# Moving the block transpose of head 16 behind the second MLP half of batch 0, and that of head 17 and the hash of heads 14 to 17 a little later

## The chip, the cores and the metric

One core of a Trainium2 chip runs the kernel. The metric is device time of one execution in microseconds (us), the median of several runs. A profile's span is some 1.8 us shorter than the time of the same run. Each run also lists the mean clock that was granted to TensorE (1.0 is full speed).

TensorE is the matmul engine, VectorE and ScalarE work on elements, GpSimd does elementwise work here, slowly (2.13 us for one `scale` of 128 x 768 elements), and SyncE only issues transfers, in order, from one queue.

## The reference, cut to what matters

```python
def _attn_ref(q, k, v, proj):              # batch 4, 8 heads, 768 positions, head size 64
    q_bucket, k_bucket = ...               # 6-bit hash of each row of q and of k, by the signs of x @ proj
    scores = scale * q @ k.T               # masked to -1e9 where the two buckets differ
    return softmax(scores) @ v

def _moe_ref(x, w_in, w_out):              # 3072 tokens, 512 -> 2048 -> 512
    h = x @ w_in
    return (h * cos(h)) @ w_out
```

So attention is followed by a dense MLP. The kernel numbers the heads of all batches 0 to 31; batch 0 is heads 0 to 7, batch 1 heads 8 to 15, batch 2 heads 16 to 23.

## The kernel before: the parts that matter

The program is one fixed interleaving of all work. Step `s` does the scores of slot `s` and the attention sums of slot `s - 1`, in nine units. Other work is hung onto this clock by `at(time, f, ...)`: 10.5 means behind unit 4 of step 10. This orders the instructions of every engine's queue; it sets no time.

```python
    PREP.update({hd: hd - 5.6 for hd in range(16, 28)})
    PREP[16] = 10.5                                  # head 17: 11.4
    HASH = {10: 8.2, 14: 12.4, 18: 16.4, ...}        # cut
    ...
    for m in range(8, NH // 2):                      # loads of heads 2m and 2m+1
        at(9.05 if m == 8 else PREP[2 * m] - 2.6, load_qk, m)      # SyncE queue
        at(9.1 if m == 8 else PREP[2 * m] - 2.4, load_v, m)
    for hd in range(H, NH):
        at(SCALE.get(hd, PREP[hd]), scale, hd, nc.vector if hd == 8 else nc.gpsimd)
        at(PREP[hd], blocks, hd)                     # VectorE
        at({...}.get(hd, SCALE.get(hd, PREP[hd]) + 0.12), turn, hd)   # DMA transpose, SyncE queue
```

`blocks(hd)` is one VectorE transpose in 32 x 32 blocks of the loaded q and k; only the hash reads its result. `scale(hd)` makes a bf16 copy on GpSimd, which `turn(hd)` transposes by DMA. The hash of four heads is 16 small matmuls.

Twice per batch, at the head of a step, stands an MLP half. For batch 0 the second one, `hidden(0, 1)`, opens step 11:

```python
    def hidden(b, c, pools):                         # pools: ps_o (2 buffers) and ps_st (3), in turn
        for ff in range(NFF):                        # 16 groups
            hp = pool.tile([P, 512], FP32, ...)      # PSUM
            for ft in range(NFT): nc.tensor.matmul(out=hp[:, 0:TOK], ...)     # 4 matmuls, 384 columns
            nc.scalar.activation(out=cs, in_=hp[:, 0:TOK], func=ACTF.Sin, ...)
            nc.vector.tensor_tensor(out=gt, in0=hp[:, 0:TOK], in1=cs, op=ALU.mult)   # the gate

    def normalize(s):                                # VectorE: flat, osum, rec, xtok
        ...                                          # osum reads the last use of a ps_o buffer
```

The two `ps_o` buffers ("o_att") also hold the attention sums. `normalize(9)` stands at the end of step 10, so VectorE gets `blocks(16)` (10.5), then `normalize(9)`, then the 16 gates of `hidden(0, 1)`, in this order.

The softmax here doesn't subtract the row's maximum and nothing guards it: scores larger than these inputs give would overflow.

## Time and profile before

| before | |
|---|---|
| time, median of 3 runs | 314.02 us (313.32 to 314.09) |
| span of the profile | 311.6 us |
| TensorE busy | 300.9 us (97%) |
| span before the second MLP half of batch 0 | 78.16 us |
| this half (16 groups) | 15.43 us |
| span after it | 218.01 us |

The half's limits are the start of its first matmul (line 485) and the start of the first attention matmul behind it (line 371).

TensorE is nearly always busy, so only places where it is not can give much. This is the view of busy time by stretch for the kernel before, cut at the half. Columns: stretch and its length, then busy us (and instructions) of TensorE, its weight loads, VectorE, ScalarE, GpSimd, then granted TensorE clock, DMA share, GB/s.

```profile
78.16:93.59 15.43, 12.40 (x65) 6.81 (x65) 9.66 (x19) 9.30 (x18) 11.29 (x10) 0.89 0.94 253
93.59:311.60 218.01, 213.14 (x1927) 126.74 (x1925) 123.54 (x247) 168.96 (x315) 50.10 (x43) 1.00 0.32 84
```

Three of 15.4 us are idle, and the mean clock is 0.89. The waits between 70 and 100 us (who waited for whom: total, times, longest) say what for:

```profile
DVE qk L224 <- DMA nat_qk<-in_k_dram: 5.7, 1, 5.7
...
ACT cs L493 <- DVE gt L497: 3.1, 1, 3.1
PE o_att L485 <- DVE osum L405: 2.6, 1, 2.6
...
PE st L485 <- DVE gt L497: 0.5, 1, 0.5
```

TensorE (PE) waits for VectorE (DVE), and VectorE for the load of k. VectorE's instructions in order of time (start, us, instruction, and in brackets the idle time before it) show why one transpose matters:

```profile
75.34 0.70 DVE L288 COPY ext<-ext 8x1536 bf16<-8x1536 bf16 x1
81.73 0.98 DVE L224 STREAM_TRANSPOSE qk<-nat_qk 128x768 f32<-128x768 f32 x1 [5.69 <-DMA nat_qk<-in_k_dram]
82.63 0.19 DVE L403 COPY flat<-o_att 128x65 f32<-128x65 f32 x1
82.86 0.56 DVE L405 TENSOR_TENSOR osum<-o_att,flat 128x390 f32<-128x390 f32 x1
...
84.16 0.55 DVE L497 TENSOR_TENSOR gt<-st,cs 128x384 f16<-128x384 f32 x1
```

The transpose of head 16 waits 5.69 us for its load, and flat, osum and the gates stand behind it. Nothing overtakes. The Trainium skill, "TensorE: Matmul & The Clock Gate" (the table at its head), calls the queues of VectorE, ScalarE and GpSimd "8 strict FIFO"; for VectorE this trace agrees: the attention matmuls that flat reads had ended by 77.1 us, and flat ran at 82.63, behind the transpose.

TensorE's instructions in the same form, and below them the chain of waits (start, us, what):

```profile
79.46 1.46 PE L485 MATMUL st<-xT,win 128*128 128x384 f16 x8
83.47 0.81 PE L485 MATMUL o_att<-xT,win 128*128 128x384 f16 x4 [2.55 <-DVE osum L405]
84.76 1.08 PE L485 MATMUL st<-xT,win 128*128 128x384 f16 x4 [0.48 <-DVE gt L497]
```

```profile
77.26 4.38 DMA nat_qk<-in_k_dram
...
81.73 0.98 DVE qk L224
82.71 0.12 DVE flat L403
...
84.24 0.48 DVE gt L497
...
84.76 1.08 PE st L485 x4
```

Four groups go through; the fifth needs an o_att buffer, which osum must first read. Last, the clock, again by stretch (the third column from the right):

```profile
84.00:85.00 1.00, 0.52 (x4) 0.23 (x3) 1.00 (x3) 0.20 (x1) 1.00 (x2) 1.00 1.05 372
85.00:86.00 1.00, 1.00 (x6) 0.46 (x5) 1.00 (x3) 0.88 (x3) 0.92 (x2) 0.58 1.10 381
86.00:87.00 1.00, 1.00 (x5) 0.50 (x4) 1.00 (x3) 0.37 (x1) 0.87 (x2) 0.50 1.06 246
87.00:88.00 1.00, 1.00 (x5) 0.50 (x4) 0.34 (x2) 0.49 (x1) 0.96 (x1) 0.50 1.27 189
88.00:89.00 1.00, 1.00 (x6) 0.51 (x5) 0.28 (x2) 0.49 (x1) 1.00 (x1) 0.71 0.97 320
```

TensorE counts as fully busy here, but at half speed. Sixteen groups at 0.65 us (four matmuls of 384 columns, back to back) are 10.4 us; 15.43 less 10.4 less 2.55 less 0.48 leaves 2.0 us. Of these, the clock column accounts for some 1.7 (0.42, 0.50, 0.50 and 0.29 of the four stretches from 85 to 89 us).

### The profile page before, as it was taken

The page shows a single profiled execution, that of the slowest core. Times are in us where ns is not written, and L with a number is a line of the kernel's source. Part 1 is how long each engine was busy: PE and PEld are TensorE (multiplying, and loading weights), DVE is VectorE, ACT ScalarE, POOL GpSimd, SP SyncE. Part 2 cuts the span into 40 slices and gives each one's busy share as a digit, 9 for nine tenths or more (in the row PEclk, how much of TensorE's full clock was granted, in tenths as well). Part 3 has the DMA queues.
Part 4 walks back from the last instruction along what each step waited for, and adds up shares of the span by engine and source line. Part 5 has one row for each costly group of instructions (what it writes and reads, how often), then busy time and mean ns, then how long its engine had stood idle before and what let it go on. Part 6 is the DMA issues. An engine that isn't in the chain of part 4 may idle for free.

```text
span 311.6 us, 7060 instructions
## 1 busy us (share of the span) xinstructions
PE 300.9 (97%) x2782; PEld 181.6 (58%) x2782; DVE 190.9 (61%) x371; ACT 243.9 (78%) x457; POOL 125.3 (40%) x134
## 2 busy tenths in 40 slices
PE   8999999999599999999999999999999999999995
PEld 2587665656356565656655656665656655654542
DVE  3788967966478877658856676539851265130720
ACT  3789998989569898997787978998768886942821
POOL 4697996899599357704931830000000000000000
PEclk9999999999989999999999999999999999999999
DMA  6679999956982479349407352340001200123001
GB/s 199 233 138 281 251 178 194 322 111 132 304 197 97 98 218 199 93 84 313 75 2 219 90 86 74 69 108 2 2 0 56 69 32 23 47 54 101 34 36 67
DMA packets 53569, 38.07 MB, mean 122 GB/s; under 512 B 33600, under 2 KB 49312, under 8 KB 53536
## 3 DMA queue, kind: packets, MB, share of 16 engines
q1 hardware_dynamic: 44272, 26.99, 34.2%
q0 software_dynamic: 8320, 10.49, 14.9%
q8 instruction: 22, 0.36, 0.5%
q10 hardware_dynamic: 944, 0.13, 0.3%
q14 instruction: 11, 0.09, 0.1%
HBM read 27.27 MB, written 6.29 MB: 108 GB/s over the span
## 4 chain that ended last, share of the span: by engine, by line
PE 69%; DMA 12%; POOL 10%; issue 3%; SPq 2%; DVE 2%; ACT 1%; POOLq 0%; ACTq 0%; DVEq 0%
PE y L509 22%; PE st L328 13%; PE st L485 12%; PE o_att L485 8%; PE o_att L371 8%; DMA nat_v<-in_v_dram 4%; DMA nat_qk<-in_k_dram 4%; DMA wout<-in_moe_w_out_dram 3%; POOL blk L205 2%; PE tp L509 2%; PE tp L234 2%; POOL vacc L126 2%; POOL v_ext L121 1%; SPq L87 1%; POOL wout L469 1%
## 5 line engine op out<-in xcount | busy, mean ns | idle before, releaser
L336 ACT ACTIVATE pt<-st 128x512 f16<-128x512 f32 x288 | 154.6, 617 | 19.8 <-PE st L328 18.6
L509 PE MATMUL y<-wout,gt 128*128 128x512 f16 x352 | 109.3, 378 | 0.0
L328 PE MATMUL st<-ext 72*128 72x512 bf16 (+3 forms) x480 | 108.0, 294 | 0.9 <-DVE ext L169 0.6
L371 PEld LDWEIGHTS <-pt 128*128 128x128 f16 x1152 | 71.1, 97 | 27.6
L371 PE MATMUL o_att<-v_ext,pt 128*128 128x65 f16 x1152 | 82.1, 193 | 0.0
L485 PEld LDWEIGHTS <-win 128*128 128x128 f16 x512 | 50.6, 99 | 39.3 <-issue 7.5
L205 POOL TENSOR_SCALAR blk<-nat_qk 128x768 bf16<-128x768 f32 x23 | 50.7, 2203 | 41.4 <-DMA nat_qk<-in_k_dram 27.4
L328 PEld LDWEIGHTS <-ext 72*128 72x128 bf16 x480 | 43.9, 97 | 30.3 <-issue 7.3
L485 PE MATMUL st<-xT,win 128*128 128x384 f16 x304 | 59.0, 330 | 0.6 <-DVE gt L497 0.5
L497 DVE TENSOR_TENSOR gt<-st,cs 128x384 f16<-128x384 f32 x76 | 41.7, 555 | 16.9 <-ACT cs L493 12.3
L493 ACT ACTIVATE cs<-st 128x384 f16<-128x384 f32 x76 | 37.1, 491 | 12.5 <-PE st L485 8.9
L485 PE MATMUL o_att<-xT,win 128*128 128x384 f16 x208 | 43.0, 330 | 3.8 <-DVE osum L405 2.6
L509 PEld LDWEIGHTS <-gt 128*128 128x128 f16 x384 | 33.6, 98 | 14.0
L497 DVE TENSOR_TENSOR gt<-o_att,cs 128x384 f16<-128x384 f32 x52 | 28.9, 555 | 12.6 <-ACT cs L493 9.8
L405 DVE TENSOR_TENSOR osum<-o_att,flat 128x390 f32<-128x390 f32 x24 | 13.6, 565 | 33.1 <-PE o_att L371 32.5
L493 ACT ACTIVATE cs<-o_att 128x384 f16<-128x384 f32 x52 | 25.5, 491 | 6.3 <-PE o_att L485 6.2
L224 DVE STREAM_TRANSPOSE qk<-nat_qk 128x768 f32<-128x768 f32 x24 | 23.1, 969 | 5.9 <-DMA nat_qk<-in_k_dram 5.7
L524 ACT COPY o_sb<-y 128x512 f32<-128x512 f32 x22 | 12.8, 583 | 14.6 <-PE y L509 14.6
L126 POOL TENSOR_TENSOR vacc<-nat_v 128x384 f32<-128x384 f32 x16 | 17.0, 1063 | 0.0
L121 POOL CAST v_ext<-nat_v 128x768 f16<-128x768 f32 x16 | 13.6, 848 | 5.9 <-PE o_att L371 2.7
L422 DVE TENSOR_TENSOR xtok<-osum,rec 128x384 f16<-128x384 f32 x24 | 15.3, 638 | 0.9
L169 DVE TENSOR_SCALAR ext<-qk 64x768 bf16<-64x768 f32 x15 | 14.5, 968 | 0.4
(78 smaller groups left out, 183.1 us busy)
## 6 DMA issues: line engine op xcount, KB each, us to landing
out_dram<-o_sb SPq DMA_DIRECT2D x23, 256.0 KB
nat_qk<-in_q_dram SPq DMA_DIRECT2D x10, 384.0 KB
nat_qk<-in_k_dram SPq DMA_DIRECT2D x10, 384.0 KB
nat_v<-in_v_dram SPq DMA_DIRECT2D x10, 384.0 KB
nat_v<-in_v_dram POOLq DMA_DIRECT2D x6, 384.0 KB, 8.5
win<-in_moe_w_in_dram POOLq DMA_DIRECT2D x8, 256.0 KB, 9.7
wout<-in_moe_w_out_dram POOLq DMA_DIRECT2D x8, 256.0 KB, 7.9
nat_qk<-in_q_dram POOLq DMA_DIRECT2D x5, 384.0 KB, 8.6
```

The source lines that it names most:

```text
L121: nc.gpsimd.tensor_copy(out=v_all[:, a:a + 2, 0:SB, 0:D], in_=x.rearrange("p h (t d) -> p h t d", d=D),)
L126: nc.gpsimd.tensor_add(acc, x[:, :, 0:3 * D], x[:, :, 3 * D:6 * D])
L205: engine.tensor_scalar(out=blk[hd].rearrange("p t w d -> p w t d"), in0=nat[hd].rearrange("p w (t d) -> p w t d", d=D), scalar1=QK_PRESCAL ...
L224: nc.vector.transpose(out=f32[hd].rearrange("p w c -> p (w c)"), in_=nat[hd].rearrange("p w c -> p (w c)"),)
L328: nc.tensor.matmul(out=st[:, o:o + n], lhsT=e[:, 1, jt * P:(jt + 1) * P], rhs=e[:, 0, t0 * P + c:t0 * P + c + n], start=True, stop=True,)
L336: nc.scalar.activation(out=pts[s][:, u * UNIT:(u + 1) * UNIT], in_=st, func=ACTF.Exp, bias=EXP_BIAS, scale=EXP_SCALE,)
L371: nc.tensor.matmul(out=o_state[s][:, qt * VW:(qt + 1) * VW], lhsT=pts[s][:, f:f + P], rhs=v_all[:, hd % NV, token(hd // H, jt)], start=(i ...
L422: nc.vector.tensor_tensor(out=xtok[b][:, t0:t0 + nt, h * D:(h + n) * D].rearrange("p t (n d) -> p n t d", n=n), in0=o_ps[:, :, 0:D].rearra ...
L485: nc.tensor.matmul(out=hp[:, 0:TOK], lhsT=win_t[ft][:, ff * P // WC, ff * P % WC:ff * P % WC + P], rhs=xT[b, c][:, ft], start=(ft == 0), s ...
L493: nc.scalar.activation(out=cs, in_=hp[:, 0:TOK], func=ACTF.Sin, bias=math.pi / 2.0, scale=1.0)
L497: nc.vector.tensor_tensor(out=gt, in0=hp[:, 0:TOK], in1=cs, op=ALU.mult)
L509: nc.tensor.matmul(out=y_state[b, t], lhsT=gates[b, c][ff][:, tt * P:(tt + 1) * P], rhs=wout_t[:, ff], start=(ff == 0), stop=(ff == NFF - 1),)
```

## The change

The intent is that nothing in front of the MLP half's normalisation and gates waits for the load of heads 16 and 17. The whole diff:

```diff
     PREP.update({hd: hd - 5.6 for hd in range(16, 28)})
-    PREP[16] = 10.5
+    PREP.update({16: 11.05, 17: 11.5})
     PREP.update({28: 22.0, 29: 22.5, 30: 23.0, 31: 23.5})
     PLACE = {10: 8.3, 11: 8.4, 12: 9.8, 13: 10.0}
-    HASH = {10: 8.2, 14: 12.4, 18: 16.4, 22: 20.4, 26: 23.4, 30: 24.6}
+    HASH = {10: 8.2, 14: 12.7, 18: 16.4, 22: 20.4, 26: 23.4, 30: 24.6}
```

`blocks`, `scale` and `turn` of head 16 go from step 10 into step 11, whose MLP half is emitted before its units. Those of head 17 move by one unit; they, like the hash, stood behind that half already. The hash of 14 to 17 moves from unit 4 to unit 6 of step 12, and with it the placements of its bits and the copies of heads 16 and 17 that must precede them (`split`). No instruction is added or removed; the queues of ScalarE and GpSimd keep their order.

## The prediction

> **What bounds the kernel now.** The page: TensorE 300.9 us busy of a 311.6 us span (97%). By stretches, TensorE is busy from 94 to 276 us but for about 1 us. The one large hole is 78 to 94 us (12.86 us busy of 16), in the second MLP half of batch 0 (line 485, emitted at step 11). There the chain of waits runs through the load of heads 16 and 17: its K half is issued at 77.26 us and lands at 81.7. `blocks(16)` is emitted at step 10.5, so it stands in VectorE's in-order queue ahead of the normalisation of step 9 (flat, osum, rec, xtok) and of every gate multiply. VectorE stands still for 5.69 us until the load lands (waits: "qk L224 <- DMA nat_qk", once), and makes the first gate at 84.16. TensorE has done four groups of the half by about 80.9 and waits 2.55 us for osum, to get an accumulator buffer, and 0.48 us for a gate.
>
> A second cost follows: the granted clock drops to 0.50 to 0.58 from 85 to 88 us and is back at 1.0 by 89. The Trainium skill ("TensorE: Matmul & The Clock Gate", "The HAM clock gate") says that an idle window of about 3.4 us halves the clock and a busy one restores it; this trace agrees (some 3.5 us at half clock, after about 3 us of idle time). The other MLP halves, with idle times of at most 0.5 us, keep 1.0. So this half takes 78.16 to 93.6 = 15.4 us, where 16 groups at 0.65 us make 10.4.
>
> **What the change does.** Nothing is added or removed. `blocks(16)` (0.98 us VectorE), `scale(16)` (2.13 us GpSimd) and its DMA transpose move from step 10.5 to unit 0 of step 11, behind the MLP half in program order; those of head 17 move one unit later; the hash of 14 to 17 (1.43 us TensorE) moves two units, its placements with it. The load keeps its place in its queue and still lands near 81.7; nobody urgent waits for it.
>
> **On the critical path.** Up to about 80.9 us nothing changes. Then osum is done near 78 instead of 83.4, so the fifth group starts at once. The sixth needs the first gate: the first cosine starts at 80.40 behind the table load, 0.49 + 0.56 us make 81.5, a stall of 0.1 to 0.2 us. The clock stays up. The half should end at about 88.8 instead of 93.6: a gain of 4.8 us = 2.55 + 0.48 + about 1.8 of half clock. Given back: 0.98 us of VectorE after the half, where it idles 0.99 us before the next flat, so nothing. Settling head 14 keeps about 1 us of slack behind its later placement. From there on TensorE binds, so the gain should reach the end.
>
> **Prediction:** 309.2 us (-1.5%), range 308.3 to 310.8. Faster by over 2%: 0.03; within 2%: 0.96; slower: 0.01.
>
> **What would show it.** Right: no VectorE wait of microseconds on the load; no TensorE wait for osum; granted clock 1.0 in 78 to 90; MLP half of about 10.6 us; span about 306.8; `scale(16)` still at about 81.8. Wrong: a TensorE gap of over 1 us in the half or a low clock there; a new VectorE wait at the settling of 14; TensorE waiting for blocks before the hash; a new stall after 89 us.
>
> **What would make it wrong.** The clock dip may not come from the idle time and stay (gain about 3 us); the transposes to features may start the half later; TensorE, 5 us earlier, may catch up with loads in the SyncE queue, whose waits before 92 us did not depend on it.

## The result, and the profile after

| | before | after |
|---|---|---|
| time, median of 4 runs | 313.67 us (313.18 to 314.09) | 309.52 us (309.12 to 310.18) |
| span of the profile | 311.6 | 308.4 |
| before the half | 78.16 | 79.85 |
| the half | 15.43 | 10.52 |
| after the half | 218.01 | 218.03 |

The ratio is 0.987, with a 95% interval of 0.9845 to 0.9896. By the threshold of 2% that is "same", and it is clear of noise.

The views of after that answer those above: the stretches,

```profile
79.85:90.37 10.52, 10.52 (x64) 6.25 (x64) 7.74 (x15) 9.18 (x18) 8.13 (x7) 1.00 1.18 301
90.37:308.40 218.03, 213.15 (x1928) 126.75 (x1925) 124.31 (x248) 168.74 (x315) 54.59 (x47) 1.00 0.34 87
```

the waits between 70 and 100 us, where the matmuls' only entry is 0.2 us and the load is waited for by GpSimd alone (with its instruction from the view in order of time),

```profile
POOL blk L205 <- DMA nat_qk<-in_k_dram: 2.1, 1, 2.1
...
PE st L328 <- ACT pt L336: 0.2, 1, 0.2
```

```profile
83.23 2.13 POOL L205 TENSOR_SCALAR blk<-nat_qk 128x768 bf16<-128x768 f32 x1 [2.09 <-DMA nat_qk<-in_k_dram]
```

VectorE,

```profile
78.77 0.23 DVE L403 COPY flat<-o_att 128x65 f32<-128x65 f32 x1 [0.69 <-PE o_att L371]
79.03 0.56 DVE L405 TENSOR_TENSOR osum<-o_att,flat 128x390 f32<-128x390 f32 x1
...
82.61 0.56 DVE L497 TENSOR_TENSOR gt<-st,cs 128x384 f16<-128x384 f32 x1 [2.20 <-ACT cs L493]
...
91.57 0.97 DVE L224 STREAM_TRANSPOSE qk<-nat_qk 128x768 f32<-128x768 f32 x1
...
92.92 0.98 DVE L224 STREAM_TRANSPOSE qk<-nat_qk 128x768 f32<-128x768 f32 x1
...
95.66 0.23 DVE L403 COPY flat<-o_att 128x65 f32<-128x65 f32 x1 [0.16 <-PE o_att L371]
```

and TensorE:

```profile
81.15 1.46 PE L485 MATMUL st<-xT,win 128*128 128x384 f16 x8
82.45 0.81 PE L485 MATMUL o_att<-xT,win 128*128 128x384 f16 x4
83.22 0.81 PE L485 MATMUL st<-xT,win 128*128 128x384 f16 x4
```

The fifth group follows at once. Both transposes stand behind the last gate, find their data there, and only use up VectorE's idle time before the next flat (0.99 us before, 0.16 us after). The chain of waits at this place is now TensorE's own groups:

```profile
79.85 0.81 PE st L485 x4
80.66 0.65 PE o_att L485 x4
81.31 1.30 PE st L485 x8
82.61 0.65 PE o_att L485 x4
```

The clock stays at 1.00 in every stretch of the half, as in these two:

```profile
85.00:86.00 1.00, 1.00 (x9) 0.60 (x7) 1.00 (x4) 0.70 (x2) 0.94 (x2) 1.00 1.33 270
86.00:87.00 1.00, 1.00 (x8) 0.61 (x7) 0.91 (x2) 0.82 (x2) 1.00 (x2) 1.00 0.97 340
```

The half is 4.91 us shorter, but the span only 3.2 us, since this execution reached the half 1.69 us later. That part of the two programs is the same up to the middle of step 10; in the profiles of the first eight experiments (three of them with a moved load) it took 78.3 to 79.7 us in seven and 81.8 in e7's, which had a slow clock earlier. So it varies without this change; why is open. It hides part of the gain in this pair of profiles.

### The profile page after: what moved, and what is told of

The parts are those of the page before. It is cut to its first block, busy times and chain, and to the rows that moved or that the text cites. A ratio compares the mean times of both kernels' runs of the same rounds, so it can differ in the third digit from the quotient of the medians.

```text
span 308.4 us, 7059 instructions
## 1 busy us (share of the span) xinstructions
PE 299.6 (97%) x2782; PEld 181.3 (59%) x2782; DVE 190.0 (62%) x371; ACT 243.5 (79%) x457; POOL 125.7 (41%) x134
## 4 chain that ended last, share of the span: by engine, by line
PE 67%; DMA 10%; POOL 8%; ACT 5%; SPq 3%; issue 3%; DVE 3%; POOLq 0%; ACTq 0%; DVEq 0%
PE y L509 21%; PE st L485 13%; PE st L328 12%; PE o_att L485 9%; PE o_att L371 7%; DMA nat_v<-in_v_dram 5%; ACT pt L336 4%; DMA nat_qk<-in_k_dram 4%; PE tp L234 2%; PE tp L509 2%; SPq L434 2%; POOL wout L469 1%; POOL vacc L126 1%; POOL nat_qk L87 1%; DMA xT<-xtok 1%
## 5 line engine op out<-in xcount | busy, mean ns | idle before, releaser
L205 POOL TENSOR_SCALAR blk<-nat_qk 128x768 bf16<-128x768 f32 x23 | 50.0, 2175 | 35.0 <-DMA nat_qk<-in_k_dram 17.2
L485 PE MATMUL st<-xT,win 128*128 128x384 f16 x304 | 57.9, 326 | 0.1
L485 PE MATMUL o_att<-xT,win 128*128 128x384 f16 x208 | 42.3, 326 | 2.0 <-DVE gt L497 2.0
L126 POOL TENSOR_TENSOR vacc<-nat_v 128x384 f32<-128x384 f32 x16 | 17.9, 1116 | 0.0
L220 DVE COPY ext<-ext 64x768 bf16<-64x768 bf16 x24 | 9.7, 423 | 8.7 <-DMA ext<-blk 8.4
```

The source lines that it names most:

```text
L126: nc.gpsimd.tensor_add(acc, x[:, :, 0:3 * D], x[:, :, 3 * D:6 * D])
L205: engine.tensor_scalar(out=blk[hd].rearrange("p t w d -> p w t d"), in0=nat[hd].rearrange("p w (t d) -> p w t d", d=D), scalar1=QK_PRESCAL ...
L485: nc.tensor.matmul(out=hp[:, 0:TOK], lhsT=win_t[ft][:, ff * P // WC, ff * P % WC:ff * P % WC + P], rhs=xT[b, c][:, ft], start=(ft == 0), s ...
```

## The experiments

Theory A: all of the gain is the half. VectorE's wait for the load, handed on to TensorE, is taken away, and with it the idle time that brought the half clock. Rivals: R1, the gain is in the moved hash and the new order of the SyncE queue; R2, the later hash is needed; R3, the 0.98 us of the transpose costs, not its wait; R4, the clock falls for another reason than idle time. Unless said otherwise each kernel was run six times, beside eleven runs of the kernel before on the same chip. All results were correct.

### The changed kernel again

No edit.

> The changed kernel again, in more rounds, to pin the size of the gain: the four runs so far gave 4.1 us, where the profiles of the MLP half alone give 4.9 us (15.4 us before, 10.5 after). Theory A (the whole gain is the half: VectorE's wait for the load of heads 16 and 17 taken out from in front of the normalisation and the gates): ratio 0.984 to 0.987, half of 10.4 to 10.7 us, clock 1.0 through it. Theory B (part of it is given back by the later hash and placements): the stretch from the end of the half to the end of the span is longer than before's 218.0 us by 0.5 us or more.

Measured: 308.72 us (308.62 to 310.31) against 312.51 (311.06 to 314.41): ratio 0.9883 (0.985 to 0.9915). The half took 10.52 us, the rest of the span 218.0 us: nothing is given back, and theory B falls. But the gain is smaller than 4.9 us, just outside the expected ratio, and the kernel before is the one whose clocks scatter, from 0.992 to 1.0.

### Only the VectorE transpose of head 16 moved

```diff
-        at(PREP[hd], blocks, hd)
+        at(11.05 if hd == 16 else PREP[hd], blocks, hd)      # in the kernel before
```

> Kernel before, with only the VectorE block transpose of head 16 moved behind the MLP half (step 11.05); its GpSimd scaling, its DMA transpose, head 17 and the hash stay. Theory A: the whole gain, ratio equal to that of the full change within 0.003, half of about 10.5 us, no VectorE wait on the load. Rival R1 (the gain is in the hash of 14 to 17 and the order of the SyncE queue that moved with it): ratio 0.997 to 1.003.

Measured: 309.51 us (308.78 to 309.82), ratio 0.9892 (0.9861 to 0.9923), half 10.40 us. Of the waits between 70 and 100 us, only this one is for the load:

```profile
POOL blk L205 <- DMA nat_qk<-in_k_dram: 5.7, 1, 5.7
```

The move of one instruction has the whole gain within noise.

### All of the change but that

```diff
-        at(PREP[hd], blocks, hd)
+        at(10.5 if hd == 16 else PREP[hd], blocks, hd)       # in the changed kernel
```

> The changed kernel with only the block transpose of head 16 put back to step 10.5: all else of the change stays (scaling and DMA transpose of 16, all of 17, hash and placements). Theory A: no gain, ratio 0.998 to 1.002, VectorE waits 5 to 6 us on the load again and TensorE 2 to 3 us on osum, with a clock dip after it. Rival R1: ratio about 0.987.

Measured: 313.41 us (311.06 to 314.0), ratio 1.0019 (0.9981 to 1.0056). No gain, so R1 falls. But the profiled run, the fastest of the six, did not look as expected. Waits between 70 and 100 us of this kernel:

```profile
DVE qk L224 <- DMA nat_qk<-in_k_dram: 4.2, 1, 4.2
...
PE st L485 <- DVE gt L497: 0.5, 1, 0.5
...
PE o_att L485 <- DVE osum L405: 0.3, 1, 0.3
```

VectorE waited 4.2 us, TensorE only 0.3, the clock stayed at 1.0, and the half took 11.48 us. The expected waits (5 to 6 and 2 to 3 us) and the dip were missed in this profile. So the damage done by the same program order differs from run to run.

### The changed kernel with the hash put back

```diff
-    HASH = {10: 8.2, 14: 12.7, ...
+    HASH = {10: 8.2, 14: 12.4, ...
```

> The changed kernel with the hash of 14 to 17 put back to step 12.4. Theory A: same as the changed kernel within 0.2% (ratio 0.984 to 0.989); the hash's move is no source of gain, at most TensorE waits some tenths of a microsecond before the hash for a block transpose that now comes later. Rival R2 (the later hash is needed, as head 17's blocks would hold TensorE at the hash): 1 us or more of TensorE wait before the hash and a ratio of 0.990 or more.

Measured: 309.28 us (308.69 to 310.06), ratio 0.9892 (0.9861 to 0.9924); half 10.52 us, rest 218.2 us. The expected 0.9890 is missed by the last digit, with the changed kernel itself at 0.9883 in these rounds. No matmul waits for a block transpose before the hash in this profile, where R2 expected 1 us or more. R2 falls: the hash's move neither gains nor is needed.

### The load earlier, the transpose where it was

```diff
-        at(9.05 if m == 8 else PREP[2 * m] - 2.6, load_qk, m)
+        at(8.1 if m == 8 else PREP[2 * m] - 2.6, load_qk, m)     # in the kernel before
```

> Kernel before, with only the load of heads 16 and 17 issued at step 8.1 instead of 9.05, ahead of the placements of 10 to 13 in the SyncE queue; the block transpose of 16 stays at step 10.5. Theory A (it is the wait for the load, not the position of the transpose as such): the same gain as the change, ratio 0.984 to 0.989, half of 10.4 to 10.8 us, VectorE wait on the load 0 to 0.5 us. Rival R3 (the 0.98 us transpose itself in front of the gates is what costs): ratio 0.996 or more.

Measured: 309.17 us (308.51 to 309.64), ratio 0.987 (0.9838 to 0.9902). The load's K half was issued at 61.85 us, the transpose ran without waiting, and the half took 10.39 us:

```profile
76.64 0.98 DVE L224 STREAM_TRANSPOSE qk<-nat_qk 128x768 f32<-128x768 f32 x1
```

The transpose stood in front of osum and the gates as before and cost nothing: R3 falls. It is the wait in a queue, and it can be cured at either end.

### The load later

```diff
-        at(9.05 if m == 8 else PREP[2 * m] - 2.6, load_qk, m)
+        at(9.7 if m == 8 else PREP[2 * m] - 2.6, load_qk, m)     # in the kernel before
```

> Kernel before, with the same load issued later, at step 9.7, behind one DMA transpose and the load of V (1.2 and 0.55 us of issue by the trace). The dose the other way. Theory A: the load lands 2 to 3 us later, TensorE's wait for osum grows from 2.55 to 4.5 to 5.5 us, time up by 2 to 3 us: ratio 1.005 to 1.011, half of 17.4 to 18.5 us. Rivals R1 and R3: ratio 0.998 to 1.002.

Measured: 316.56 us (316.02 to 319.24), ratio 1.0127 (1.0085 to 1.0169), clock 0.987 to 0.989 in all six runs, half 18.15 us. The half is as expected; the wait for osum (6.1 us, expected at most 5.5) and the ratio (at most 1.011) are above. Its waits, and three stretches of its half:

```profile
DVE qk L224 <- DMA nat_qk<-in_k_dram: 9.6, 1, 9.6
...
PE o_att L485 <- DVE osum L405: 6.1, 1, 6.1
```

```profile
82.00:83.00 1.00, 0.00 (x0) 0.00 (x0) 0.00 (x0) 0.07 (x1) 0.00 (x0) 1.00 0.96 243
...
84.00:85.00 1.00, 0.00 (x0) 0.00 (x0) 0.00 (x0) 0.00 (x0) 0.00 (x0) 0.50 1.89 132
...
89.00:90.00 1.00, 1.00 (x4) 0.44 (x3) 1.00 (x3) 0.84 (x2) 0.96 (x2) 0.50 1.27 303
```

The clock falls while TensorE still waits and stays low for some 3 us of its work. The same kernel in other rounds, on another chip:

> The late load of e5 once more, to compare with e8 on one chip. Ratio 1.009 to 1.016, clock 0.987 to 0.989 in all runs (its idle time of 6.1 us is far longer than before's).

Measured: 315.77 us (314.94 to 316.83), ratio 1.010 (1.0052 to 1.0148), clock 0.988 to 0.995 in the six, where 0.987 to 0.989 was expected: a miss. In its profile TensorE waited 3.91 us for osum, and the half took 16.21 us. So the dose acts as theory A says, with its size again depending on the run.

### TensorE kept busy while it waits

```diff
         for ff in range(NFF):
+            if (b, c, ff) == (0, 1, 4):                 # behind the fourth group, in the kernel before
+                wp = ps_t.tile([P, 512], FP32, name="tp", space=PSUM)
+                for _ in range(11):
+                    nc.tensor.matmul(out=wp, lhsT=delta, rhs=warm.to_broadcast([P, 512]), start=True, stop=True)
```

(`warm` is also declared earlier. Nobody reads `wp`, and results stay right.)

> Kernel before, with 11 matmuls of 512 columns that nobody reads (2.4 us at 0.216 us each) put behind the fourth group of the MLP half, so that TensorE is busy while it waits for osum; results unchanged. It separates the clock from the wait. Theory A (the half clock from 85 to 88 us follows from the idle time): clock stays at 1.0 or nearly, wait for osum itself stays, half falls from 15.4 to about 13.6 us, ratio 0.993 to 0.996. Rival R4 (the dip comes from something else, as the load or the gates): dip stays, ratio 0.999 to 1.002.

Measured: 312.48 us (312.11 to 313.88), ratio 0.9982 (0.9948 to 1.0016). The clock was 0.998 to 1.0 in all six runs, beside 8 of 11 runs of the kernel before at 0.995 or less in the same rounds. In the profile the matmuls ended about 84.0, TensorE waited 0.25 us more for osum, the clock read 1.00 throughout, and the half took 13.84 us. The clock is as expected. The time is a miss: 0.993 to 0.996 was expected, and it is not told from no change.

The late load makes the dip surer, so the same was tried there, with 27 matmuls:

> The late load with 27 unread matmuls of 512 columns (5.8 us) in TensorE's wait for osum. Here the dip came in all six runs without filler, so the clock can be told from the wait more sharply than in e6. Theory A (half clock follows from TensorE's idle time): no dip in any run (clock 0.997 or more), the wait itself stays, half 16.5 to 17.0 us instead of 18.1, time 1.2 to 1.8 us below e9's. Rival R4 (the dip comes from the load, the late gates or something else than idle time): the dip stays, time as e9's within 0.5 us.

Measured: 315.53 us (314.76 to 317.62), ratio 1.0095 (1.0044 to 1.0146); clock 0.997 to 1.0 in five runs, 0.989 in one. The time did not fall: a miss. In the profile osum was done at 85.4 us, but the 27 matmuls held TensorE until 88.1; the half took 16.27 us, as e9's 16.21. Fewer of them, 16:

> e8 with 16 unread matmuls (3.45 us) instead of 27 (5.8 us). In e8's profile the 27 ended at 88.1 us, some 2.6 us after osum was done, and held TensorE longer than the wait would have; so e8's time said nothing of the clock. With 16 the filler ends before osum in every run (the waits seen were 3.9 and 6.1 us). Theory A: clock 0.997 or more in all or nearly all runs, half of 14.4 to 16.9 us and shorter than e5's and e9's by about the 1.5 to 1.8 us that the half clock costs, ratio 1.003 to 1.009 where e9 gave 1.010 and e5 1.0127. Rival R4: clock 0.987 to 0.995 as in e5 and e9, ratio 1.010 to 1.013.

Measured: 316.0 us (315.66 to 320.06), ratio 1.0137 (1.0075 to 1.0199); clock 0.997 to 1.0 in four runs, 0.992 and 0.995 in two. The time is a miss again. In its profile VectorE waited 9.2 us for the load:

```profile
DVE qk L225 <- DMA nat_qk<-in_k_dram: 9.2, 1, 9.2
...
PE o_att L492 <- DVE osum L406: 2.4, 1, 2.4
```

TensorE's 3.43 us of unread matmuls and 2.4 us of waiting are nearly e5's 6.1 us, and the half took 17.06 us at full clock, against e5's 18.15 us with the dip. (In this profile the rest took 219.1 us, 1.1 more than usual; a later wait of 1.4 us on a feature transpose is in it, and why is open.)

Taken together: with the late load and no filler, 12 of 12 runs had a clock of 0.995 or less; with filler, 3 of 12; with filler in the kernel before, 0 of 6. Idle time of TensorE causes the dip, and R4 falls as its main cause. What the dip costs in time is not shown by these ratios: the wait for the load differs by over 2 us between runs and buries it. It can be estimated inside each profile. Take from the half its 10.4 us of matmuls, the delay of its fifth group (how much later than 2.6 us after the start of the half it starts, for wait and filler together) and the wait for the first gate. What is left is 0.0 to 0.2 us in the five profiles without a dip in the half (b1 below, e2, e6, e8, e10), and 1.5 to 1.8 us in the three with one (before, e9, e5). So a dip here costs about 1.5 us by this estimate, close to the prediction's 1.8. The three runs with filler and a low clock have no profile; where their dip lay is open.

### The kernel before again, for a second profile

No edit.

> The kernel before itself, for a second profile of it and for more runs with their clocks. In the 22 runs of it beside the first eight experiments, 14 had a mean clock of 0.995 or less and 8 of 0.998 or more. Theory A2 (A, but the half clock does not come in every execution[...]): ratio 0.998 to 1.002; again part of the runs at 0.995 or less and part at 0.998 or more, the former slower by 1 to 2 us; half between 12.5 and 15.5 us in the profile, the stretch after it 218.0 us. Theory A as predicted: all runs with the dip, half of 15.4 us.

Measured: 312.25 us (310.36 to 313.04), ratio 0.9987 (0.9934 to 1.0041). The profiled run took 310.36 us, and this is its half, with VectorE's and TensorE's wait:

```profile
79.54:90.55 11.01, 10.56 (x65) 6.24 (x65) 9.49 (x19) 9.27 (x18) 9.69 (x8) 1.00 1.02 240
```

```profile
DVE qk L224 <- DMA nat_qk<-in_k_dram: 3.8, 1, 3.8
...
PE st L485 <- DVE gt L497: 0.4, 1, 0.4
```

The unchanged kernel passes the half in 11.01 us, under the expected 12.5, with no wait for osum and no dip. With the clocks of the other runs this is A2; A as predicted, the same loss in every execution, falls.

### Both cures at once

The changed kernel with the load at step 8.1.

> The changed kernel with the early load of e4 as well. Theory A: nobody urgent waits for this load any more, so nothing further: ratio within 0.002 of the changed kernel's. If the load was still holding something after the change (scaling of 16 on GpSimd, which waited 2 us for it), up to 0.5% better.

Measured, in eight runs: 309.64 us (308.61 to 312.37), ratio 0.9879 (0.9842 to 0.9915). Nothing further. Its profiled run, at 312.12 us, had a half of 10.52 us like the others, but a half clock far earlier (from 39 to 50 us; the moved load was issued at 61), and reached the half only at 81.83. Another run took 312.37 us at a clock of 1.0. Both are open, so slow executions of other causes remain. No version here beats the changed kernel; the early load alone equals it.

## Why the prediction was right

The time was 309.5 us against 309.2 predicted, and the steps named came as said: no wait of VectorE for the load, none of TensorE for osum, full clock, and 0.12 us of stall before the sixth group (0.1 to 0.2 predicted). Not as said are the absolute times in the profile: this execution came to the half 1.69 us later, so its span was 308.4 us, not 306.8, and `scale(16)` began at 83.23 us, not 81.8. (a0's profile has the 306.8.)

- **The cause.** Shown. One VectorE instruction, `blocks(16)`, carries the gain: moved alone, ratio 0.9892; left behind alone, 1.0019. With its data there in time it costs nothing in the old place: 0.987. Nor was the load merely in time by luck where the transpose had been moved: GpSimd, which still waits for it, got it 2.1 to 4.1 us after the start of the half (after, a0, e1, e3), for which the rule below gives 1.2 to 3.2 us of wait in the old order. TensorE waited for none of it.
- **The half.** Predicted about 10.6 us, measured 10.52, with no wait for osum and clock 1.0.
- **Nothing given back.** The rest of the span is 218.0 us before and after, and within 0.4 us of that in eleven of the twelve experiment profiles; the other is e10's, 219.1 us. VectorE's idle time took the transpose, as predicted.
- **The size** was too high as an average. "A gain of 4.8 us = 2.55 + 0.48 + about 1.8 of half clock" is what one execution lost. The gain was 4.15 us by the medians of the first runs, and 3.5 us over all runs: the mean of 49 runs of the kernel before in the four sets of rounds and in b1 is 312.8 us, that of the 10 runs of the changed one (the first four and a0's six) 309.3. (A fiftieth run, of 315.79 us, was slow and is left out.) The terms that were mis-sized are the wait and the half clock, both read as fixed. That the first gain came within 0.7 us of the forecast is in part luck: the four runs of the kernel before beside it, 313.18 to 314.09 us, all lie above that mean.
- **The reason for the half clock.** The prediction also said that this trace agrees with the skill's idle window of about 3.4 us. No stretch of 3.4 us was idle here, only 2.55 and 0.48 us with 0.8 us of work between. That the dip follows idle time is shown by the filler runs; the rule for how much is not.

The wait is a race. By the trace before, osum is done 1.7 us after the load lands and the transpose starts (81.73 to 83.43), and TensorE wants the buffer four groups, 2.6 us, after the half starts. So its wait should be the landing less the start of the half, less 0.9 us:

| profile | half starts | transpose starts | estimated wait | wait measured | half |
|---|---|---|---|---|---|
| b1 (before) | 79.54 | 80.37 | 0 | 0 | 11.01 |
| e2 | 79.71 | 81.01 | 0.4 | 0.3 | 11.48 |
| before | 78.16 | 81.73 | 2.7 | 2.55 | 15.43 |
| e9 (load late) | 79.75 | 84.68 | 4.0 | 3.91 | 16.21 |
| e5 (load late) | 78.68 | 85.81 | 6.2 | 6.11 | 18.15 |

(The row "before" gave the 0.9; the others test it.) From before to b1 the transpose's start comes 2.7 us nearer to the start of the half: the half began 1.4 us later, the load was issued 0.9 us earlier, and it took 0.5 us less from issue to use. So it is mostly TensorE and the SyncE queue that drift against each other; why is open. The profile used for the prediction was of an execution at the bad end.

The half clock is not fixed either. Of the 49 runs, 27 had a mean clock of 0.995 or less and a mean time of 313.5 us; 22 had 0.998 or more and 311.9 us; none lay between. (Half clock for 3.4 us of 311 lowers the mean by 0.0055.) That these 27 had their dip in this half is inferred, as only profiles show where it lies; in the 36 runs of the kernels without this wait (after, a0, e1, e3, e4, e7) one had such a clock, e7's with its early dip. The 1.6 us between the two groups is not the price of the dip alone, since long waits and dips come together. The changed kernel's ten runs have 0.998 or more, and lie within 1.7 us (308.62 to 310.31), where the 49 of the kernel before lie within 4.5 (310.24 to 314.75): the change took out an accident, not a fixed cost.

## What to carry to other kernels

In an in-order queue, an instruction whose data may be late belongs behind everything that TensorE waits for, even where its own work is under 1 us; or its load belongs earlier, which did the same here. A stall that ends a race between a transfer and an engine has no single size: look at several executions, and at each run's mean clock, before putting one profile's microseconds into a sum. Filling idle time with unread work kept the clock in 15 of 18 runs here, but gained no time that could be told from noise, and where it outlasted the wait (e8) it took the wait's place.

## What the Trainium skill lacked or had wrong

- "TensorE: Matmul & The Clock Gate" ("The HAM clock gate") has the clock halve after an idle window of about 3.4 us, and its closing table warns of idle gaps over about 3 us. Here 2.55 us of waiting and another 0.48 us after 0.8 us of work were enough in one execution (0.50 to 0.58 from 85 to 88 us), while 2.39 and 0.48 us in e10's profile were not. So idle time cut up by work, no piece of it as long as the page's figures, can be enough.
- The same page says that the window is free-running, and that the number of slow matmuls at a kernel's start therefore varies between runs. It does not say that a dip in mid-kernel can come and go between executions of one program: here the mean clock suggests it in 27 of 49 runs, and of two profiles of the kernel before one has it and one has not.
- It agrees on size and duration: half clock, for about 3.4 us after a wait of 2.55 us, for about 3.4 us after one of 3.91 us in e9, and for about 6.8 us (83.7 to 90.6 us) around one of 6.1 us in e5.
- No page says how far the time from issue to landing of one and the same load scatters between executions of a program. With the same issue order, the K half of this load took 4.0 us (b1) and 4.5 us (before) from issue to the start of the waiting transpose; with the late load it took 5.1 to 5.9 us in four profiles (e5, e8, e9, e10).
